# Attention and channel mix on one core: a longer search for the order of the work, and half as many dummy products

## The chip, the cores and the metric

The kernel runs on one core of one Trainium2 chip. The time is the device time of one execution, in microseconds (us). A core has five engines that run side by side, each with its own queue and strictly in that queue's order: PE (matrix products), ACT (functions of one operand, copies), DVE (elementwise work with two operands, scans), POOL (small side work) and SP (here it only starts transfers). PE shows twice in the profile: PE is the product, PEld the loading of its stationary operand.

## The reference

The first part is a linear attention with a decaying state: 4 batches, 8 heads, 768 steps, head size 48. The second part mixes each step with the one before it and sends it through a gated two-layer network with 384 features and 1,024 hidden ones.

```python
for t in range(S):
    state = alpha[:, :, t, :, None] * state + np.einsum('bhd,bhe->bhde', k[:, :, t], v[:, :, t])
    y[:, :, t] = np.einsum('bhd,bhde->bhe', q[:, :, t], state)
...
xk = mu_k * x + (1.0 - mu_k) * x_prev
xr = mu_r * x + (1.0 - mu_r) * x_prev
k = np.maximum(xk @ w_k, 0.0)
v = k * k @ w_v
r = 1.0 / (1.0 + np.exp(-(xr @ w_r)))
return (r * v).astype(np.float32)
```

All in float32; `x` is `y` with the heads side by side.

## The kernel before

**Tiles and stages.** The 768 steps of each batch are cut into chunks of 128, and the chunks into nine groups (`CUTS`, line 27): three groups of two chunks for the first batch, two groups of three for each of the others. A chunk of a group is called a unit; there are 24. For each group the kernel loads four tiles (`al`, `q`, `k`, `v`; two buffers each), runs the decay forward and backward over the group with two scans on DVE (`fwd`, line 357, and `bwd`, line 381), and multiplies q and k by them (`qm`, `km`, line 398). For each unit PE transposes k (`trans`, line 448), ACT copies the result (`keep`, line 455), and PE makes a visit (line 582): one visit finishes one unit (its products inside the chunk, and those with the old state) and starts the next (its state update and its scores). Behind a visit DVE masks the scores (`masked`, line 472) and advances the state (`advance`, line 535), ACT copies the output (`copied`) and DVE adds to it (`crossed`). Two small transfers (`moved`, line 575) complete the group's output.

Then follows the network for the group: ACT and DVE mix the steps and split the result into a high and a low part (`mix_*`, lines 604 to 620), PE makes eight first-layer products (`up`, line 628), each passed on by ACT (`relu`, `square`, `high`) and DVE (`low`); one gate product for each chunk (`gate`, line 657); and eight second-layer products for each chunk (`down`, line 672). Each product is three: high by high, high by low, low by high. The weights come in ten pieces, each split by ACT and DVE before use (`split_*`, lines 309 to 347), and four of them land in buffers that group tiles use later.

**What sets the order.** The kernel writes down all this work as jobs (line 68): engine, price in us (`COST`, line 48), what it depends on, and which buffer it opens or frees. The class `Plan` (line 63) then lays the jobs out on the host, while the program is built. `forward` (line 97) goes through time and gives each engine the ready job with the earliest latest-time; a transfer of a given size is priced by `RATE` and `LAND` (line 56). `backward` (line 155) goes from the end and gives each job the latest time at which it can start without moving the end; buffers that the forward pass found shared count as dependencies. `solve` (line 193) takes turns with both, 12 times (`PASSES`), and keeps the start times of the shortest layout. Each job has a `rank` that is added to its latest time, and it is 0 for every job. The loads are tied in a fixed order among themselves; `moved` and the stores find their own places among them in SP's queue.

The loop at line 1021 issues the jobs of all five engines in the order of the planned start times. Where the plan leaves PE empty for more than 0.7 us before a PE job, and that job starts before 60 us (`EARLY`) of the plan, it puts dummy products in front of it: `dummy(m)` (line 444) issues m products of a zero tile into a spare corner of the transposes' PSUM tile. So a dummy waits for that tile, and the next transposes wait behind the dummies.

Of the kernel before, what the change touches and what calls it, by code (L numbers as in the profile page):

```python
# [43 lines left out]
NX = HB - D  # L44
MERGE = ()
EARLY = 60.0
PASSES = 12
COST = {
    "fwd": (2.4, 3.45), "bwd": (2.32, 3.38), "am": 0.62, "adv": 0.72, "scl": 0.4, "cross": 0.42,
# [13 lines left out]
class Plan:  # L63
# [129 lines left out]
    def solve(self):  # L193
        jobs = self.jobs
        self.links = self.users()
        self.holders = {}
        for k, j in jobs.items():
            for o in j["frees"]:
                self.holders.setdefault(o, []).append(k)
        late = self.backward({k: j["n"] for k, j in jobs.items()}, ())  # L200
        best = None
        for _ in range(PASSES):
            ranked = {k: t + jobs[k]["rank"] for k, t in late.items()}
            start, span, edges = self.forward(ranked)
            self.spans = getattr(self, "spans", []) + [span]
            if best is None or span < best[0]:
                best = (span, start)
            late = self.backward(start, edges)
        self.end = {k: t + jobs[k]["cost"] for k, t in best[1].items()}
        return sorted((t, jobs[k]["n"], k) for k, t in best[1].items())  # L210

# [2 lines left out]
def gated_attention_channel_mix(  # L214
# [225 lines left out]
    def room(name):  # L440
        spare[0] = ps.tile([C, 512], F32, tag="pt", name=name)
        return spare[0][:, : NP * R].rearrange("c (p r) -> c p r", p=NP)

    def dummy(m):
        for _ in range(m):
            PE.matmul(spare[0][:R, NP * R :], zero, zero[:, : 512 - NP * R], start=True, stop=True)  # L446
# [569 lines left out]
    with tc.manual_schedule(engines={ET.PE, ET.SP, ET.Activation, ET.DVE, ET.Pool}):  # L1016
        nc.scalar.dma_start(mu, mu_p)
        DVE.tensor_scalar(nu, mu, -1.0, 1.0, op0=ALU.mult, op1=ALU.add)
        room("warm")
        busy = 0.9  # L1020
        for t, _, key in plan.solve():
            j = plan.jobs[key]
            if j["eng"] == "PE":
                if t < EARLY and t - busy > 0.7:
                    dummy(int((t - busy - 0.4) / 0.2))
                busy = t + j["cost"]
            j["fn"]()

# [2 lines left out]
    with tc.If(good < R):  # L1031
# [11 lines left out]
        with tc.For_i(0, S, TB) as t0:  # L1043
            a, k, q = (p1.tile([128, TB, DW], F32, tag=n, name="f" + n) for n in ("xrh", "pp", "kh"))
# [162 lines left out]
```

## Time and profile before

| | |
|---|---|
| time, three runs | 387.15, 388.81, 395.81 us (median 388.81) |
| the profiled execution's own time | 387.16 us |
| its span, first to last instruction | 385.4 us |
| mean granted PE clock | 0.952 |
| PE busy | 366.7 us, 95% |
| DVE busy | 240.8 us, 62% |
| ACT busy | 213.1 us, 55% |
| of PE: line 446, the dummies (76 and 246 records) | 14.4 and 35.1 us |

The page lists busy time by engine, the span in 40 equal slices with the busy share in tenths, the chain of work that ended last, and the costliest groups of instructions by line. The row PEclk gives the clock that PE was granted, in tenths. A timeline row gives start, length, engine, line and operation, output and inputs, shapes and count, and in brackets how long the engine stood idle before it and what ended that. Consecutive products overlap, so the length of one is more than the distance to the next.

### The profile page before, as it was taken

Reading aid. Unit: us, or ns where it says so; the run is one execution under the profiler, and the core shown is the slowest. Engines: PE = TensorE matmul, PEld = TensorE weight load, DVE = VectorE, ACT = ScalarE, POOL = GpSimd, SP = SyncE. Lnnn points to the kernel's source line nnn. Section 1 sums busy time; section 2 is a strip of 40 time slices with the busy share of each in tenths; the row PEclk is TensorE's granted clock in tenths of the full one; section 3 lists DMA queues with packets and bytes.
Section 4 is the critical chain, followed back from the end, with each engine's and each line's share of the span. In section 5 each row is a group of like instructions: output and inputs, shape, how many; then the busy total and the mean of one; then the engine's idle time right before and its main releaser. Section 6 shows DMA issues by size and latency. Waiting matters only on the chain.

```text
span 385.4 us, 11112 instructions
## 1 busy us (share of the span) xinstructions
PE 366.7 (95%) x4868; PEld 354.1 (92%) x4868; DVE 240.8 (62%) x399; ACT 213.1 (55%) x436; POOL 22.8 (6%) x54
## 2 busy tenths in 40 slices
PE   8998998988999999799999999999999999999993
PEld 8887997988899899799999999999999999999992
DVE  7459699768989797986788637523822452342210
ACT  2252694255558737648773578239717836826700
POOL 4000000100002000060002000000000000000000
PEclk9999599558999999899999999999999999999998
DMA  8930948912718119201901700010010010010001
GB/s 246 370 86 7 320 169 239 252 29 60 234 38 253 50 44 245 54 22 51 266 4 43 242 6 0 31 52 0 21 39 22 1 42 22 0 43 20 2 20 48
DMA packets 10999, 35.60 MB, mean 92 GB/s; under 512 B 1552, under 2 KB 5488, under 8 KB 10944
## 3 DMA queue, kind: packets, MB, share of 16 engines
q1 hardware_dynamic: 10800, 34.82, 29.6%
q8 instruction: 40, 0.66, 0.7%
q14 instruction: 15, 0.12, 0.1%
q10 hardware_dynamic: 144, 0.00, 0.0%
HBM read 28.92 MB, written 4.72 MB: 87 GB/s over the span
## 4 chain that ended last, share of the span: by engine, by line
PE 87%; DVE 5%; DMA 3%; issue 2%; ACT 1%; SPq 0%; DVEq 0%; ACTq 0%
PE pv L680 27%; PE pk L635 24%; PE pg L663 9%; PE pt L446 7%; PE warm L446 4%; PE sp L466 4%; PE yu L528 4%; PE yu L490 3%; PE pt L453 3%; DMA al<-al_p 3%; PE sp L510 2%; PE yu L510 2%; ACT ht L457 1%; DVE vraw L326 1%; DVE wvl L345 1%
## 5 line engine op out<-in xcount | busy, mean ns | idle before, releaser
L655 DVE TENSOR_TENSOR kl<-sq,kh 128x384 fp32r<-128x384 f32 (+1 forms) x72 | 36.1, 510 | 48.8 <-ACT kh L651 48.7
L680 PE MATMUL pv<-wvh,kh 128*128 128x384 f32 x192 | 66.4, 346 | 0.2 <-ACT r L642 0.2
L680 PE MATMUL pv<-wvl,kh 128*128 128x384 f32 x192 | 64.9, 338 | 0.0
L680 PE MATMUL pv<-wvh,kl 128*128 128x384 f32 x192 | 64.4, 335 | 0.0
L642 ACT ACTIVATE r<-pk 128x384 f32<-128x384 f32 (+1 forms) x72 | 32.7, 454 | 40.6 <-PE pk L635 40.4
L635 PE MATMUL pk<-xkh,wkh 128*128 128x384 f32 (+1 forms) x216 | 48.2, 333 | 0.0
L635 PE MATMUL pk<-xkh,wkl 128*128 128x384 f32 (+1 forms) x216 | 46.2, 323 | 0.0
L635 PE MATMUL pk<-xkl,wkh 128*128 128x384 f32 (+1 forms) x216 | 46.0, 322 | 0.0
L646 ACT ACTIVATE sq<-r 128x384 f32<-128x384 f32 (+1 forms) x72 | 35.3, 490 | 12.5 <-DVE kl L655 10.7
L446 PE MATMUL pt<-st 112*112 112x64 f32 x246 | 35.1, 315 | 3.1 <-ACT ht L457 3.1
L446 PEld LDWEIGHTS pt<-st 112*112 112x112 f32 x246 | 33.5, 227 | 4.9 <-ACT ht L457 4.4
L680 PEld LDWEIGHTS pv<-wvh,kh 128*128 128x128 f32 x192 | 36.0, 187 | 1.2 <-ACT r L642 0.5
L635 PEld LDWEIGHTS pk<-xkh,wkh 128*128 128x128 f32 x216 | 36.4, 194 | 0.7
L635 PEld LDWEIGHTS pk<-xkh,wkl 128*128 128x128 f32 x216 | 36.8, 194 | 0.0
L635 PEld LDWEIGHTS pk<-xkl,wkh 128*128 128x128 f32 x216 | 36.7, 193 | 0.0
L680 PEld LDWEIGHTS pv<-wvh,kl 128*128 128x128 f32 x192 | 36.1, 188 | 0.0
L680 PEld LDWEIGHTS pv<-wvl,kh 128*128 128x128 f32 x192 | 36.0, 188 | 0.0
L651 ACT ACTIVATE kh<-sq 128x384 fp32r<-128x384 f32 (+1 forms) x72 | 34.8, 488 | 2.0
L607 ACT ACTIVATE x<-xt,mu 128x384 f32<-128x384 f32 (+1 forms) x54 | 27.9, 571 | 13.4 <-DVE xrl L620 8.9
L686 DVE TENSOR_TENSOR sig<-pv,sig 128x384 f32<-128x384 f32 x24 | 13.3, 555 | 32.6 <-PE pv L680 32.5
L457 ACT COPY ht<-pt 128x448 f32<-128x448 f32 x24 | 12.7, 528 | 36.8 <-PE pt L453 31.4
L611 DVE SCALAR_TENSOR_TENSOR x<-xt,nu,x 128x384 f32<-128x384 f32 (+1 forms) x54 | 28.1, 568 | 3.0 <-ACT x L607 2.1
(84 smaller groups left out, 576.3 us busy)
## 6 DMA issues: line engine op xcount, KB each, us to landing
out<-sig SPq DMA_DIRECT2D x24, 192.0 KB, 1.9
al<-al_p SPq DMA_DIRECT2D x6, 673.8 KB, 11.2
q<-q_p SPq DMA_DIRECT2D x6, 672.0 KB, 5.0
k<-k_p SPq DMA_DIRECT2D x6, 672.0 KB, 7.1
v<-v_p SPq DMA_DIRECT2D x6, 600.0 KB, 9.2
both<-wk_p SPq DMA_DIRECT2D x4, 768.0 KB, 10.3
vraw<-wv_p SPq DMA_DIRECT2D x4, 768.0 KB, 7.9
al<-al_p SPq DMA_DIRECT2D x3, 449.8 KB, 5.6
```

Of the source, the lines that this page charges most:

```text
L446: PE.matmul(spare[0][:R, NP * R :], zero, zero[:, : 512 - NP * R], start=True, stop=True)
L457: ACT.copy(ht[u], pts[u])
L466: PE.matmul(sp[s * HC : (s + 1) * HC, j, p * HC : (p + 1) * HC], h[rr, c, p, tt], q[rr, c, p, tt], start=True, stop=True,)
L607: ACT.activation(mixed[g, i][:, t], xt[:, t, 1 : 1 + n], AF.Copy, scale=mu[:, i, t : t + 1])
L611: DVE.scalar_tensor_tensor(x, xt[:, t, 0:n], nu[:, i, t : t + 1], x, op0=ALU.mult, op1=ALU.add)
L635: PE.matmul(pk, w[:, t, cols], x[:, t], start=i == 0 and t == 0, stop=i == 2 and t == NT - 1,)
L642: ACT.activation(self.r[f], self.p["u", f], AF.Relu)
L646: ACT.activation(self.s[f], self.r[f], AF.Square)
L651: ACT.activation(self.k[0][:, f], self.s[f], AF.Copy)
L655: DVE.tensor_tensor(kl[:, f], self.s[f], kh[:, f].bitcast(F32), op=ALU.subtract)
L663: PE.matmul(pg, x[:, i, cols], w[:, i], start=k == 0 and i == 0, stop=k == 2 and i == NT - 1,)
L680: PE.matmul(pv, x[:, f, cols], w[:, f], start=f == 0 and i == 0, stop=f == NF - 1 and i == 2,)
```

## The change

Two things change. The planner's search gets 160 rounds in place of 12 passes. In every round but the first, each latest time is moved by a number between -30 and +30 us (`SHAKE`), from a generator with a fixed seed; the forward pass runs on these, and its result is then improved by a backward and a forward pass without shaking. Each of the two layouts is kept if it is the shortest so far by the planner's prices, and the next round shakes around the kept one. The first round is not shaken and gives the first two layouts of the kernel before. The rank is no longer added. And a planned gap on PE gets about half as many dummies: one for each 0.4 us in place of 0.2. No job, price, dependency or tile changes.

```diff
-PASSES = 12
+PASSES = 160
+SHAKE = 30.0
...
+        seed = 1
+
+        def shake():
+            nonlocal seed
+            seed = (seed * 1103515245 + 12345) % 2**31
+            return (seed / 2**30 - 1.0) * SHAKE
+
         late = self.backward({k: j["n"] for k, j in jobs.items()}, ())
         best = None
-        for _ in range(PASSES):
-            ranked = {k: t + jobs[k]["rank"] for k, t in late.items()}
-            start, span, edges = self.forward(ranked)
-            self.spans = getattr(self, "spans", []) + [span]
-            if best is None or span < best[0]:
-                best = (span, start)
-            late = self.backward(start, edges)
+        self.spans = []
+        for i in range(PASSES):
+            start, span, edges = self.forward({k: t + shake() if i else t for k, t in late.items()})
+            for _ in range(2):
+                if best is None or span < best[0]:
+                    best = (span, start)
+                    late = self.backward(start, edges)
+                if span == float("inf"):
+                    break
+                start, span, edges = self.forward(self.backward(start, edges))
+            self.spans.append(best[0])
         self.end = {k: t + jobs[k]["cost"] for k, t in best[1].items()}
         return sorted((t, jobs[k]["n"], k) for k, t in best[1].items())
...
                 if t < EARLY and t - busy > 0.7:
-                    dummy(int((t - busy - 0.4) / 0.2))
+                    dummy(int((t - busy - 0.5) / 0.4))
                 busy = t + j["cost"]
```

## The prediction

> **What bounds the kernel now.** I read the page's summary first, then the stretches ahead of and behind the first second-layer product, then the chain of waits with the timelines of PE and DVE in the first 100 us. The page's busy times, the granted clock in tenths, and the chain:
>
> ```profile
> PE 366.7 (95%) x4868; PEld 354.1 (92%) x4868; DVE 240.8 (62%) x399; ACT 213.1 (55%) x436; POOL 22.8 (6%) x54
> PEclk9999599558999999899999999999999999999998
> PE 87%; DVE 5%; DMA 3%; issue 2%; ACT 1%; SPq 0%; DVEq 0%; ACTq 0%
> ```
>
> PE is busy for 95% of the span, but part of that is filler. The first `down` product starts at 97.71 us. Start, length, instruction; then three window rows (window, length, busy time and count of PE, PEld, DVE, ACT, POOL; clock; DMA share; GB/s): all engines up to 97.7, line 446 on PE alone in the same stretch, and PE from there to the end.
>
> ```profile
> 97.71 0.44 PE L680 MATMUL pv<-wvh,kh 128*128 128x384 f32 x1
> 0.00:97.70 97.70, 89.48 (x1264) 84.89 (x1264) 74.64 (x105) 47.50 (x85) 8.59 (x34) 0.84 0.58 179
> 0.00:97.70 97.70, 49.60 (x322) 0.84 0.58 179
> 97.70:385.40 287.70, 277.18 (x3608) 0.99 0.21 63
> ```
>
> Line 446 is the dummy product: 49.60 of the 89.48 us are filler, and only 39.9 us are the kernel's own. From 97.7 on PE works 277.18 of 287.70 us at 0.99 of its clock with no filler at all. So the kernel is a PE-bound stretch of 288 us behind a start-up of 98 us, and neither half of the change can shorten the PE work of that stretch: what is to be had lies in the start-up.
>
> How long one dummy takes decides the rest. The tile view counts the dummies, the chain of waits has three trains of them:
>
> ```profile
> L446 PE MATMUL warm<-st x76: 394/394/449, 1.2 to 15.3; 112*112 112x64 f32 x76
> 1.22 14.45 PE warm L446 x76
> 27.57 4.89 PE pt L446 x48
> 68.39 10.60 PE pt L446 x56
> ```
>
> Every train has an even count; I read one call of the loop as two records (one fp32 product in two passes). Then the first train is 38 calls in 14.45 us, 0.38 us each; the second 24 calls in 4.89, 0.20 each; the third 28 in 10.60, 0.38 each. The old rule puts one call per 0.2 us of planned gap: right at the fast rate, and twice the gap at the slow one. In those two slow trains filler overruns its gap and holds up real work, because PE runs in order.
>
> **The change, part by part: the dummies.** The new rule is one call per 0.4 us. If the order stayed, a count of n would mean a gap of 0.2n+0.4 to 0.2n+0.6, and so 38, 2, 5, 13 and 28 calls become 18 or 19, none or 1, 2, 6 and 13 or 14. The trains that come ahead of real work, on PE:
>
> ```profile
> 15.77 0.98 PE L453 MATMUL pt<-ident,k 112*128 112x112 f32 x4
> 17.38 1.01 PE L446 MATMUL pt<-st 112*112 112x64 f32 x4 [0.62 <-ACT ht L457]
> 21.82 2.13 PE L446 MATMUL pt<-st 112*112 112x64 f32 x10 [0.62 <-ACT ht L457]
> 39.44 5.11 PE L446 MATMUL pt<-st 112*112 112x64 f32 x26
> ```
>
> And DVE, whose bracket gives idle time and what ended it:
>
> ```profile
> 5.17 2.30 DVE L362 TENSOR_TENSOR_SCAN pp<-al,fl 112x1028 f32<-112x1028 f32 x1 [0.56 <-DMA al<-al_p]
> 10.12 0.69 DVE L398 TENSOR_TENSOR k<-k,al 112x512 f32<-112x512 f32 x1
> 18.32 0.96 DVE L326 SCALAR_TENSOR_TENSOR both<-both,tops 128x768 uint32<-128x768 uint32 x1 [5.70 <-ACT tops L315]
> 27.64 0.69 DVE L475 TENSOR_TENSOR am<-sp,mask 128x512 f32<-128x512 f32 x1 [3.22 <-PE sp L466]
> 48.25 0.69 DVE L475 TENSOR_TENSOR am<-sp,mask 128x512 f32<-128x512 f32 x1 [2.23 <-PE sp L466]
> ```
>
> Head: the transposes at 15.77 need only the k product that ended at 10.81. Nineteen calls at 0.38 end at 8.4, so they start at about 10.9: 4.9 us. The four records at 17.38 nearly go (0.6 to 1.0, I take 0.9), the ten at 21.82 become four (1.3). Together 7.1 us by the masking at 27.64, in front of which DVE stood idle for PE. Does a load take it back? DVE's split at 18.32 stands ahead of the first masking in its queue, and waits through ACT for the first weight piece:
>
> ```profile
> 2.69 0.68 SPq L303 DMA_DIRECT2D both<-wk_p  x1
> both<-wk_p SPq DMA_DIRECT2D x1, 768.0 KB, 8.4
> ```
>
> Issued at 2.69 and landing 8.4 later, it is there at 11.1: not the bound at 12 or 13 us either. So 7.1 stands.
>
> Second: 26 records become 12, 2.7 us less; the masking behind that visit waits 2.23, and work queued on DVE limits the gain to that: 2.2.
>
> Third: 56 records become 26 or 28, 5.3 to 5.7 us less. The visit behind them needs a v load; an al load holds ACT. Their issues and landings (last figure, us), the visit, and the masking that follows it:
>
> ```profile
> 60.15 0.37 SPq L291 DMA_DIRECT2D v<-v_p  x1
> v<-v_p SPq DMA_DIRECT2D x1, 400.0 KB, 6.6
> 66.47 0.31 SPq L273 DMA_DIRECT2D al<-al_p  x1
> al<-al_p SPq DMA_DIRECT2D x1, 673.8 KB, 13.9
> 79.00 1.06 PE sp L466 x32
> 80.13 0.69 DVE L475 TENSOR_TENSOR am<-sp,mask 128x512 f32<-128x512 f32 x1 [3.17 <-PE sp L466]
> ```
>
> The v load is there at 66.75, well ahead of the visit at 79.00, so the visit is free to come earlier, and DVE's idle 3.17 is the most that it brings. The al load lands only at 80.4, and ACT's queue stands behind it: the least is 0, and I take half, 1.6. Dummies: 7.1 + 2.2 + 1.6 = 10.9 us.
>
> **The clock, which pays for it.** The PE rows of two bright stretches, all PE work with DVE, and line 446 alone:
>
> ```profile
> 27.70:37.90 10.20, 8.91 (x146) 8.18 (x149) 9.99 (x16) 2.54 (x6) 0.64 (x4) 1.00 0.01 2
> 48.20:68.60 20.40, 18.25 (x216) 17.31 (x216) 19.29 (x27) 14.90 (x28) 0.46 (x4) 1.00 0.70 207
> 27.70:37.90 10.20, 6.56 (x62) 1.00 0.01 2
> 48.20:68.60 20.40, 9.64 (x90) 1.00 0.70 207
> 34.50:37.92 3.42, 2.13 (x26) 0.99 0.00 0
> 68.60:72.00 3.40, 3.40 (x20) 0.50 1.01 244
> ```
>
> Dummies that follow real work run at clock 1.00, those at 68.6 at 0.50 although PE has no gap. (In the page's first slices the clock reads 9, but the 0.38 us a call there is that of the half rate; I go by the durations.) With half of them the clock may fall sooner. Real work in the two stretches is 2.35 + 8.61 = 11.0 us, so at half clock it costs 0 to 11 us. DVE is busy 9.99 of 10.20 and 19.29 of 20.40 there and hides all but its idle 1.3: I take 1.
>
> The Trainium skill (TensorE: Matmul & The Clock Gate, "Why this matters for your kernels") wants no PE idle gap above some 3 us and says that about 4 us of sustained products bring the clock up; by that rule halved filler is a mistake, the whole 11 us would be lost, and the sum below would be 382 (the clock rival). This trace half disagrees: 14.45 us of unbroken dummies stayed at 0.38 us a call and 10.60 us did so again, so here filler does not raise the clock; that it holds a raised one (the train at 27.57) fits the rule.
>
> **The new order.** The search changes the order in every queue: PE, ACT, DVE, POOL, and on SP the places of `moved` and `store` among the loads, whose own order is fixed. No operation is added, no tile changes, the rank that is dropped was 0 everywhere. The kept plan is the shortest by the planner's own prices, so the trace has to say what an order can bring. Ceiling: DVE does work for groups 3 and 4 ahead of the first `down` that nothing of group 0 needs:
>
> ```profile
> 69.65 3.37 DVE L362 TENSOR_TENSOR_SCAN pp<-al,fl 112x1540 f32<-112x1540 f32 x1 [1.77 <-DMA al<-al_p]
> 73.15 1.27 DVE L398 TENSOR_TENSOR q<-q,pp 112x512 f32<-112x512 f32 x2
> 81.61 3.36 DVE L384 TENSOR_TENSOR_SCAN al<-al,fl 112x1540 f32<-112x1540 f32 x1
> 88.75 3.36 DVE L362 TENSOR_TENSOR_SCAN pp<-al,fl 112x1540 f32<-112x1540 f32 x1
> 94.72 3.36 DVE L384 TENSOR_TENSOR_SCAN al<-al,fl 112x1540 f32<-112x1540 f32 x1
> ```
>
> Four scans, 13.5 us, and six products at 0.635, 3.8: 17 us could move behind. Floor: the planner reckons 0.34 MB/us and 2.1 us of landing (line 56), 4.1 us for an al load of 0.674 MB, where the row above has 13.9; one such load moved onto DVE's path costs 9.8. Between -17 and +10 I take -5, nearest to the idle time that DVE has left: 97.7 - 74.64 = 23.1, less 5.2 ahead of its first scan, less 10.9 counted above, is 7, of which the load waits (1.77 before the scan at 69.65) will stay.
>
> **Sum**, against the profiled execution's own 387.16 (the median of the three runs, 388.81, is 0.4% above it): 387.16 - 10.9 - 5 + 1 = 372.
>
> **Rivals.**
> - Ceiling: the order moves the whole 17 us. 387.2 - 10.9 - 17 + 1 = 360. For it: DVE is full from 48 to 68 us, so that what it does first decides. Against: behind 97.7 PE lacks 287.7 - 277.2 = 10.5 us as it is, and scans moved there must open no new gap. Chance 0.12.
> - The search does nothing: its first two candidates repeat the old ones unshaken, and if no shaken one is shorter, the old order stays with fewer dummies: 387.2 - 10.9 + 1 = 377. Chance 0.09.
> - Clock: the halved trains let it fall at once and all 11 us lie on the path: 372 + 10 = 382. For it: in the 3.42 us ahead of 37.92, after which the page shows a 5, PE was still busy for 2.13, so a clock can fall at 62% busy. Against: DVE's full rows. Chance 0.13.
> - Hidden: the freed PE time is eaten by ACT and loads at the second and third train and half of the head: 387.2 - 3.5 = 384. Against it: the idle rows of DVE above name PE. Chance 0.08.
> - Slower: loads. A planner that believes 4.1 us for a load of 13.9 packs DVE's scans against them, and DVE, in order, stands with everything behind it. At the 9.8 us missing per load, three loads (groups 3 to 8 have this size) make 372 + 29 = 401. It decides from 25 us of load waits on DVE's and ACT's path. For it: the landing row; against: loads keep their order, and of the scans quoted just one waits, 1.77. Chance 0.11.
>
> **Numbers.** Forecast 372, chance 0.47, its own range 362 to 380 (the third train 0 or 3.2, the order 0 to -12, the clock up to 5). A measurement of this kernel tells about 2% from no change, 381.0 and 396.6. Faster: forecast, ceiling and unchanged order, 0.68. Within: clock and hidden, 0.21. Slower: 0.11. From 359 to 386 all but the slower case and edges is held.
>
> **What would show it.** PE: the opening train ends near 8 us and the first transposes stand at about 11, not 15.77. DVE: the idle 3.22, 2.23 and 3.17 in front of the maskings mostly gone. The first `down` at 80 to 84 us instead of 97.7, line 446 at well under half of 49.6 us, and about 277 us of PE work behind it as now. Clock rival: 0.50 in nearly every slice until the first `down`. Wrong: a first `down` no earlier than 95, load waits of tens of us on DVE or ACT, or new PE gaps behind 100 us.

## The result and the profile after

The changed kernel takes 364.69 us (median of four runs, 361.02 to 369.04) against 387.98 us before; the ratio is 0.936, with a 95% interval of 0.928 to 0.945. The forecast was 372 in a range from 359 to 386: the direction and the range held, and the gain is about 23 us where 16 were forecast.

Some executions of every kernel run a few per cent longer, the first profiled one after among them, so the ratios leave these out while the medians hold them, and the rows "after" below are those of a second profile of the same kernel (run `e5_after`, 367.11 us, span 365.3). In the changed kernel the lines have moved by 12: the dummies are line 458, the masking 487, the scans 374 and 396, `down` 692.

The summary of the page:

```profile
span 365.3 us, 10693 instructions
PE 338.4 (93%) x4666; PEld 324.3 (89%) x4666; DVE 239.4 (66%) x399; ACT 211.2 (58%) x436; POOL 16.1 (4%) x54
PEclk9965869999999989999989999999999999999998
```

Before, PE was busy 366.7 of 385.4 us, now 338.4 of 365.3. Line 458 on PE alone, and then all of PE, in the first 100 us (window, length, busy time and count, clock, DMA share, GB/s); the last two rows are the same pair of the kernel before:

```profile
0.00:100.00 100.00, 20.79 (x120) 0.88 0.65 198
0.00:100.00 100.00, 88.02 (x1366) 0.88 0.65 198
0.00:100.00 100.00, 49.60 (x322) 0.85 0.59 182
0.00:100.00 100.00, 91.78 (x1277) 0.85 0.59 182
```

There is no filler behind 100 us in either. So the 20.1 us between the spans are: filler 49.6 to 20.8, -28.8; PE's own work (busy time less filler) 317.1 to 317.6, +0.5; PE idle 18.7 to 26.9, +8.2. And of its own work PE has done 67.2 us by 100 us, where it had done 42.2: 25 us more. Of these 25, five are lost again behind 100 us, nearly all as PE idle time, 10.5 us before and 14.9 now.

The timeline of PE and DVE after, with the rows that answer to those of the prediction: the opening train, the first transposes, the first `down`, the second masking, and the scans of groups 3 and 4.

```profile
1.22 6.98 PE L458 MATMUL warm<-st 112*112 112x64 f32 x36 [1.22 <-DVE st L727]
10.85 0.98 PE L465 MATMUL pt<-ident,k 112*128 112x112 f32 x4 [2.64 <-DVE k L410]
59.26 0.34 PE L692 MATMUL pv<-wvh,kh 128*128 128x384 f32 x1
20.50 0.68 DVE L487 TENSOR_TENSOR am<-sp,mask 128x512 f32<-128x512 f32 x1
65.35 3.37 DVE L374 TENSOR_TENSOR_SCAN pp<-al,fl 112x1540 f32<-112x1540 f32 x1 [1.48 <-DMA al<-al_p]
69.70 3.36 DVE L396 TENSOR_TENSOR_SCAN al<-al,fl 112x1540 f32<-112x1540 f32 x1
85.19 3.37 DVE L374 TENSOR_TENSOR_SCAN pp<-al,fl 112x1540 f32<-112x1540 f32 x1
89.74 3.36 DVE L396 TENSOR_TENSOR_SCAN al<-al,fl 112x1540 f32<-112x1540 f32 x1
```

The train ends at 8.2 and the transposes start at 10.85, as soon as DVE's product is there. DVE no longer stands idle ahead of the second masking (3.22 us before). The first `down` comes at 59.3 instead of 97.7, and all four long scans, which had stood ahead of it, now stand behind it.

### The profile page after: what moved, and what is told of

Same layout as the page of the kernel before. It is cut to its first block, busy times and chain, and to the rows that moved or that the text cites. A ratio compares the mean times of both kernels' runs of the same rounds, so it can differ in the third digit from the quotient of the medians.

```text
span 367.3 us, 10693 instructions
## 1 busy us (share of the span) xinstructions
PE 341.0 (93%) x4666; PEld 327.1 (89%) x4666; DVE 239.4 (65%) x399; ACT 211.5 (58%) x436; POOL 16.7 (5%) x54
## 4 chain that ended last, share of the span: by engine, by line
PE 58%; DMA 6%; DVE 6%; issue 3%; ACT 2%; SPq 1%; DVEq 0%; ACTq 0%
PE pv L692 23%; PE pk L647 20%; PE pg L675 7%; DMA al<-al_p 5%; PE yu L502 2%; PE sp L478 2%; DVE pp L374 2%; DMA xt<-xt 2%; PE yu L540 2%; PE pt L465 1%; PE sp L522 1%; PE yu L522 1%; SPq L590 1%; DVE xt L581 1%; DVE al L396 1%
## 5 line engine op out<-in xcount | busy, mean ns | idle before, releaser
L692 PE MATMUL pv<-wvh,kh 128*128 128x384 f32 x192 | 68.3, 356 | 2.1 <-ACT sig L682 1.7
L692 PE MATMUL pv<-wvl,kh 128*128 128x384 f32 x192 | 66.0, 344 | 0.0
L692 PE MATMUL pv<-wvh,kl 128*128 128x384 f32 x192 | 65.5, 341 | 0.0
L667 DVE TENSOR_TENSOR kl<-sq,kh 128x384 fp32r<-128x384 f32 (+1 forms) x72 | 35.5, 509 | 41.3 <-ACT kh L663 41.2
L663 ACT ACTIVATE kh<-sq 128x384 fp32r<-128x384 f32 (+1 forms) x72 | 34.6, 487 | 28.5 <-PE pv L692 26.9
L647 PE MATMUL pk<-xkh,wkh 128*128 128x384 f32 (+1 forms) x216 | 49.1, 338 | 0.0
L647 PE MATMUL pk<-xkl,wkh 128*128 128x384 f32 (+1 forms) x216 | 46.9, 327 | 0.0
L647 PEld LDWEIGHTS pk<-xkh,wkh 128*128 128x128 f32 x216 | 37.2, 200 | 0.7
L647 PEld LDWEIGHTS pk<-xkh,wkl 128*128 128x128 f32 x216 | 37.8, 199 | 0.0
L623 DVE SCALAR_TENSOR_TENSOR x<-xt,nu,x 128x384 f32<-128x384 f32 (+1 forms) x54 | 29.1, 569 | 8.7 <-ACT x L619 7.9
L374 DVE TENSOR_TENSOR_SCAN pp<-al,fl 112x1540 f32<-112x1540 f32 (+1 forms) x9 | 27.1, 3007 | 1.5 <-DMA al<-al_p 1.3
L396 DVE TENSOR_TENSOR_SCAN al<-al,fl 112x1540 f32<-112x1540 f32 (+1 forms) x9 | 27.0, 3003 | 0.1
```

Source lines behind the costliest of these rows:

```text
L374: DVE.tensor_tensor_scan(flat(pp), flat(al), fl[:, : NP * (n + 1)], initial=START, op0=ALU.mult, op1=ALU.max)
L396: DVE.tensor_tensor_scan(back, back, fl[:, : NP * (n + 1)][:, ::-1], initial=0.0, op0=ALU.mult, op1=ALU.max)
L623: DVE.scalar_tensor_tensor(x, xt[:, t, 0:n], nu[:, i, t : t + 1], x, op0=ALU.mult, op1=ALU.add)
L647: PE.matmul(pk, w[:, t, cols], x[:, t], start=i == 0 and t == 0, stop=i == 2 and t == NT - 1,)
L663: ACT.activation(self.k[0][:, f], self.s[f], AF.Copy)
L667: DVE.tensor_tensor(kl[:, f], self.s[f], kh[:, f].bitcast(F32), op=ALU.subtract)
```

## The experiments

Theory A is the one of the prediction: a dummy takes 0.38 us at the slow rate, so the old trains held real work up; the rest is the order. B: the order does all of it. C: filler holds the clock, and less of it costs.

**The two halves apart, and no filler at all.** The four kernels ran together, beside a kernel before of 388.48 us.

Half the dummies, old order:

```diff
-                    dummy(int((t - busy - 0.4) / 0.2))
+                    dummy(int((t - busy - 0.5) / 0.4))
```

> The order of before with the new rule for dummies alone. Theory A (a dummy takes 0.38 us at the slow rate, so the old trains overran their gaps and held real work up, and the clock costs little): 377, the opening train over at about 8 us. Theory B (the order does all of it, freed PE time is eaten elsewhere): 384 to 388. Theory C (less filler means a slower clock on the path): 385 to 395.

Measured: 380.98 us, ratio 0.980 (0.971 to 0.989). Faster, but by 7.5 us and not 11. The maskings in the old order, line 475, now read:

```profile
19.89 0.69 DVE L475 TENSOR_TENSOR am<-sp,mask 128x512 f32<-128x512 f32 x1 [1.40 <-PE sp L466]
38.38 0.69 DVE L475 TENSOR_TENSOR am<-sp,mask 128x512 f32<-128x512 f32 x1
66.38 0.68 DVE L475 TENSOR_TENSOR am<-sp,mask 128x512 f32<-128x512 f32 x1
```

They stood at 27.64, 48.25 and 80.13: 7.8, 9.9 and 13.8 us earlier. The first `down` and PE from there to the end:

```profile
83.27 0.44 PE L680 MATMUL pv<-wvh,kh 128*128 128x384 f32 x1
83.27:380.30 297.03, 280.12 (x3608) 0.97 0.22 61
```

The first `down` came at 97.71, so 14.4 us were gained up to it. Behind it the same 3,608 records take 297.0 us where they took 287.7: 9.3 us are given back, 2.9 as busy time and 6.4 as idle time. The waits of PE say what the idle time is (total us, times, longest): this kernel first, then the kernel before.

```profile
PE pt L453 <- issue: 8.5, 3, 4.1
PE pk L635 <- issue: 2.0, 1, 2.0
PE sp L466 <- issue: 1.5, 1, 1.5
```

```profile
PE sp L510 <- issue: 2.8, 2, 2.3
PE yu L510 <- issue: 1.0, 1, 1.0
```

"Issue" is idle time for which the profile names no releaser: 12.0 us against 3.8. Not all of it is of one kind. One of these waits ends 0.1 us behind DVE's product k, which the transposes need:

```profile
26.73 0.69 DVE L398 TENSOR_TENSOR k<-k,al 112x512 f32<-112x512 f32 x1
27.52 0.98 PE L453 MATMUL pt<-ident,k 112*128 112x112 f32 x4 [1.89 <-issue]
```

The other 10.1 us, all behind the first `down`, end 1.3 to 1.5 us after a 16 KB piece of PE's code has landed, as the last section shows; I call them waits for code. In the kernel before they are all of the 3.8 us, also behind the first `down`, so they account for nearly the whole 6.4 us of idle time. That is a cost that the prediction did not have; the last runs go after it. PE's own work also took longer, 346.7 - 23.5 = 323.2 us against 317.1, at a mean clock of 0.934 against 0.952.

The new order with the old rule:

```diff
-                    dummy(int((t - busy - 0.5) / 0.4))
+                    dummy(int((t - busy - 0.4) / 0.2))
```

> The new order with the old rule for dummies. Theory A: the order brings what the dummies do not, 24 of 388 less 11, so about 375; the opening train ends at 15.7 us again. Theory B: 364, as with both. Theory C: 355 to 362, for more filler holds the clock.

Measured: 373.13 us, ratio 0.959 (0.955 to 0.963), as A has it. So the order alone is worth 15 us, the dummies alone 7.5, and both together 19 to 25 (the ratios 0.950, in a later set of runs, and 0.936): within the spread they add up. PE's own work done by 100 us adds up in much the same way: 55.7 us with half the dummies alone, 55.6 with the order alone (91.14 busy less 35.50 of filler, below), 67.2 with both, 42.2 with neither.

```profile
0.00:100.00 100.00, 35.50 (x258) 0.98 0.61 181
0.00:100.00 100.00, 91.14 (x1324) 0.98 0.61 181
```

No dummies, in the new order and in the old one:

```diff
-EARLY = 60.0
+EARLY = 0.0
```

> The new order with no dummies at all. Theory A (filler does not raise the clock and holds it only where nothing of weight runs): within 4 us of the changed kernel, 360 to 367. Theory C: 370 or more, with the clock at 0.50 for most of the first 60 us. If dummies are still in the way of real work: under 360.

> The order of before with no dummies at all. Theory A: 374 to 380, at or a little under the half-filled one. Theory C: slower than the half-filled one by 5 us or more.

Measured: 366.13 us, ratio 0.946 (0.940 to 0.951), in the new order; 373.10 us, ratio 0.961 (0.956 to 0.967), in the old. In the old order no filler at all is 8 us faster than half of it, just below the range of A, and C, which expected it slower, falls. But filler is not the whole of these 8 us: waits for code make 4.6 us here and 10.1 with half the dummies. The new order's gain with no filler in either is 7 us, less than half of the 15 that it has with the old trains. Under the old rule the new order issues 35.5 us of filler where the old one issues 49.6; that the rest of the 15 comes from this is a reading that no run tests.

**The opening train, and whether the chip follows the planner.** Four kernels beside a kernel before of 389.95 us. The first is the changed kernel again, as the measure for the others.

> The changed kernel again, as the measure for the runs beside it: 0.93 to 0.95 of the kernel before, 360 to 369 us.

Measured: 367.04 us, ratio 0.950 (0.938 to 0.962).

The changed kernel without its opening train only:

```diff
-                if t < EARLY and t - busy > 0.7:
+                if 0.9 < busy and t < EARLY and t - busy > 0.7:
```

> The changed kernel without its opening train of dummies (36 records, 6.98 us ahead of the first transposes), all later ones kept. Theory A (the opening train ends before its work is ready and does not raise the clock): the same as the changed kernel within 2 us. Theory C (the opening train readies the clock for the first visits): slower by 2 to 5 us, first visits at the slow rate for longer.

Measured: 357.91 us, ratio 0.924 (0.913 to 0.934): 9 us faster, which no theory had. The train cannot have held anything up: with it the first transposes start at 10.85, without it at

```profile
11.11 0.98 PE L465 MATMUL pt<-ident,k 112*128 112x112 f32 x4 [11.11 <-DVE k L410]
```

At 43 us the kernel with the train is even 0.8 us ahead: the next dummies start at 42.18 with it and at 42.95 without. What differs comes later. All waits on "issue" with the train, and then the only one without it:

```profile
PE sp L478 <- issue: 2.8, 2, 1.7
PE pv L692 <- issue: 1.9, 1, 1.9
PE yu L522 <- issue: 1.9, 1, 1.9
PE pt L458 <- issue: 1.6, 1, 1.6
PE pt L465 <- issue: 0.5, 1, 0.5
```

```profile
PE sp L478 <- issue: 1.8, 1, 1.8
```

8.7 us against 1.8; all but the last line of the five, 0.5 us that end 0.1 behind DVE's product k, are waits for code. One wait of 1.61 ends at 45.87, inside the dummies that started at 42.18; the nine records behind it take 0.2 us each, which is the slow rate:

```profile
45.87 1.76 PE L458 MATMUL pt<-st 112*112 112x64 f32 x9 [1.61 <-issue]
```

The page's clock row above reads 6 in the slice that begins there (the sixth of 40), and without the train it reads 9:

```profile
PEclk9975899999999999999899999999999999999997
```

PE's own work is 313.0 us without the train (325.9 busy, 12.9 of it filler) and 317.6 with it. PE from 43 us to the end, with the train and then without it, and three stretches of the kernel with the train:

```profile
43.00:365.30 322.30, 302.71 (x4077) 0.97 0.26 74
43.00:356.60 313.60, 298.79 (x4085) 0.99 0.26 76
45.30:52.10 6.80, 6.23 (x49) 0.50 0.01 4
130.60:134.00 3.40, 3.40 (x13) 0.50 0.18 63
181.80:185.20 3.40, 3.40 (x58) 0.50 0.29 98
```

So the whole 8.7 us between the two spans arise behind 43 us: 4.8 as idle time, where waits for code are 7.0 against 1.8 us, and 3.9 as busy time. Three of the four waits for code there, of 1.61, 1.86 and 1.85 us, have a stretch at half the clock upon them, 13.6 us together; without the train there is one such wait, of 1.83, and one such stretch, of 3.4, ahead of the idle end. Not every wait has one (1.71 us at 107.00 has none), and that the waits bring the stretches about is argued from their places.

Less search, and another seed:

```diff
-PASSES = 160
+PASSES = 20
```

> The changed kernel with 20 rounds of search in place of 160: the planner's own length for its plan is 353.2, between 356.1 (the order of before, which took 381.0 with half the dummies) and 344.3 (160 rounds). If the length of the plan carries over to the chip: 375 to 379. If the chip does not follow the planner and the new order was a lucky one: anywhere from 362 to 385, most likely 366 to 372.

```diff
-        seed = 1
+        seed = 7
```

> The changed kernel with another seed for the shaking (7), which gives another order, of planned length 342.7. If the length of the plan carries over: 359 to 364, a little under the changed kernel. If the new order was a lucky one: 366 to 378.

Measured: 369.67 us, ratio 0.956 (0.946 to 0.967), with 20 rounds, and 361.60 us, ratio 0.935 (0.926 to 0.945), with seed 7. Another order of nearly the same planned length is as good, so the new order was no lucky find. But 369.67 us lies in the range for a chip that does not follow the planner, and 361.60 in the one for a chip that does, and the planner's length is a poor measure: against the old order with half the dummies (0.980), the first 3 us of planned gain (356.1 to 353.2) brought 2.4 points of the ratio, the next 9 us (to 344.3) 0.6 points, and the last 1.6 (to 342.7) 1.5 points, where each ratio is known to about a point. Waits for code are 10.1, 4.2, 8.1 and 4.2 us in these four kernels, and they are not in the planner's prices.

**What the opening train does.** The last four beside a kernel before of 386.54 us. First the train with as many instructions, but 4 columns in place of 64:

```diff
-    def dummy(m):
+    def dummy(m, w=512 - NP * R):
         for _ in range(m):
-            PE.matmul(spare[0][:R, NP * R :], zero, zero[:, : 512 - NP * R], start=True, stop=True)
+            PE.matmul(spare[0][:R, NP * R : NP * R + w], zero, zero[:, :w], start=True, stop=True)
...
-                    dummy(int((t - busy - 0.5) / 0.4))
+                    dummy(int((t - busy - 0.5) / 0.4), *([4] if busy == 0.9 else []))
```

> The changed kernel, with the opening train's 18 dummies cut from 64 columns to 4: as many instructions in PE's queue, little of their time. Theory D (the opening train costs because its instructions move all later ones against the 16 KB pieces in which PE's code is fetched, so that PE stands waiting for code at other places): as the changed kernel, 0.95 of before or about 367, with 6 us or more of PE idle time put down to issue, a gap of 1.5 us or more near 46. Theory E (the train's time or its effect on the clock costs): as without the train, 0.92 or 358, at most 3 us of issue.

Measured: 366.09 us, ratio 0.947 (0.942 to 0.952), with 7.7 us of waits on "issue", 7.6 of them for code, and one ends at 46.03:

```profile
1.22 6.88 PE L458 MATMUL warm<-st 112*112 112x4 f32 x36 [1.22 <-DVE st L727]
46.03 1.00 PE L458 MATMUL pt<-st 112*112 112x64 f32 x9 [0.74 <-issue]
PEclk9999989999999999998989999999999999999999
```

The time and the sum of the waits are as D has them; the wait near 46 is half of the 1.5 us that D asked for, and the four others stand at 105 to 181 us. But the test is weaker than meant: 4 columns took 6.88 us where 64 took 6.98, so the train's time did not go. Nor does it take out the clock. The row reads 9 in the first slices, but there the durations show the slow rate: three records of `up` take 0.84 us at 38.0 and 0.52 from 39.2 on. PE's own work is 318.3 us, as with the full train. What speaks against the train's own time is that either train is over 2.6 to 3.1 us before the first transposes can start, and that next to nothing is lost up to 43 us: the dummies that start at 42.95 without a train start at 42.18 with the full one and at 43.21 with the narrow one.

> Seed 7 for the shaking, without the opening train. Seed 7 with the train waited 9.5 us for issue. Theory D: the waits fall elsewhere, with no reason for a gain: 354 to 366, the issue time moved. Theory E: 9 us faster than with the train, 352 to 354.

The edits are those of the two runs above, together. Measured: 356.65 us, ratio 0.923 (0.918 to 0.928), with 2.4 us of waits on "issue". Of the 9.5 with the train, 5.4 are one wait that ends at 32.84, 0.1 us behind DVE's product k; waits for code are 4.2 with the train and 1.9 without. The time lies in D's range and above E's; the gain of the removal is 1.2 points of the ratio here, 2.6 with seed 1.

Loads priced nearer to the trace, without the opening train:

```diff
-RATE, LAND, HOP, DRAIN, SLACK = 0.34, 2.1, 0.1, 0.25, 0.12
+RATE, LAND, HOP, DRAIN, SLACK = 0.26, 4.0, 0.1, 0.25, 0.12
```

> The changed kernel without the opening train, its planner pricing loads nearer to what the traces show (0.26 MB/us and 4.0 us of landing in place of 0.34 and 2.1). If waits for loads are what the plan lost on the chip: 350 to 355. If not: 356 to 362, no better than the same kernel with the old prices (358).

Measured: 357.22 us, ratio 0.924 (0.919 to 0.929): the same as with the old prices (0.924). Pricing loads nearer to the trace gains nothing.

Dummies that are not all zero, in the kernel before (the mask of the text below holds ones on one side of a diagonal and zeros on the other):

```diff
-            PE.matmul(spare[0][:R, NP * R :], zero, zero[:, : 512 - NP * R], start=True, stop=True)
+            PE.matmul(spare[0][:R, NP * R :], ident[:R, :R], mask[:R], start=True, stop=True)
```

> The kernel before, its dummies multiplying the identity by the mask of ones in place of zero by zero; same size and count. If zeros are why the opening train stays at 0.38 us a call: after some 4 us of the train a call takes 0.20, and the train of 76 records is over in 9 to 11 us. If the kind of product is the reason: 14.4 us as before, 388 in all.

Measured: 386.69 us, and the train as slow as ever:

```profile
2.71 14.45 PE L446 MATMUL warm<-mask,ident 112*112 112x64 f32 x76 [2.71 <-POOL mask L728]
```

So it is not that all operands are zero. Most factors still are, for the identity has one value in each column that is not; a train of dense values was not tried.

The fastest versions are the three that drop the opening train and keep the later ones, 0.923 to 0.924 of the kernel before; they differ among themselves by less than their intervals, and all are faster than the changed kernel beside which the first of them ran.

## Why the prediction was right, and where it was wrong

**Filler holds up real work: right, and its price nearly so.** The step "transposes at about 10.9" was met at 10.85, and in the old order the maskings moved by 7.8 and 9.9 us where 7.1 and 9.3 were worked out. The third step, 1.6 from a span of 0 to 3.2, was too small: the masking at 80.13 came 13.8 us earlier, so that step was about 3.9, and the al load that was to hold ACT moved forward with everything else (issued at 57.27, not 66.47). The three steps, 10.9 us, were too small for what the first `down` gained, 14.4, and too large for the total, 7.5: behind the first `down` 6.4 us more of waits for code and 2.9 more of work took back a part. The sum had no term for that; the "issue 2%" in its row of the chain showed that such waits exist.

**The order: the mis-sized term.** It was put at -5 between -17 and +10, by "nearest to the idle time that DVE has left". It measured -15 under the old rule. The choice of the nearest row was the mistake: what the search did is what the ceiling described, all four scans of groups 3 and 4 moved behind the first `down`. Two misses offset each other in part: the dummies with the clock, 9.9, were over 2 us too large, and this term 10 us too small. That the sum came within 8 us of the measured time, with no term for the waits for code, is in that part luck. Only 7 us of the 15 remain when there is no filler in either order; so the terms were also not independent of the filler.

**"The kernel is a PE-bound stretch of 288 us behind a start-up of 98 us, and neither half can shorten it": wrong as a yardstick.** The first `down` came at 59.3 us, not at 80 to 84 (with the dummies alone it came at 83.27), and what follows lasts 306 us. The first `down` is a place in the order and not the end of the start-up. The measure that adds up is PE's own work done by a fixed time: 25 us more by 100 us, 5 us lost behind it, 20 in all.

**The clock: little from before to after, more in the old order.** The term was +1. From the kernel before to the changed one PE's own work grew by 0.5 us, but in the old order with half the dummies it grew by 6.1 and with none by 3.4 (320.5 us). The two profiles of the changed kernel are 2.6 us apart (320.2 and 317.6), so only the 6.1 is clear of that. The clock rival (382) fell with the runs without any filler: the one in the old order is faster than its half-filled one, the one in the new order as fast. The Trainium skill (TensorE: Matmul & The Clock Gate, "Why this matters for your kernels") asks for no gaps above some 3 us; here 11 us of an idle PE at the start cost nothing that can be seen, while in the running kernel stretches at half the clock stood behind waits of only 1.6 to 1.9 us.

**The other rivals.** The search did find other orders. Loads: the waits of DVE and ACT for them in the changed kernel (total, times, longest):

```profile
DVE q L410 <- DMA q<-q_p: 4.1, 3, 2.6
DVE pp L374 <- DMA al<-al_p: 2.5, 3, 1.5
DVE k L410 <- DMA k<-k_p: 2.3, 3, 1.2
ACT junk L382 <- DMA al<-al_p: 11.7, 7, 2.8
ACT tops L327 <- DMA rraw<-wr_p: 1.5, 1, 1.5
```

They are 22.1 us, a little under the 25 at which the slower case was to decide, but the same waits made 18.8 in the kernel before, so the change added 3.3 and not the 29 of that case. What grew is ACT's wait for the two small transfers of `moved`, 15.1 us where it was 0.9, which no rival named.

The ceiling (360) was close: the first measurement lies halfway between it and the forecast.

## What to carry to other kernels

Before filling gaps on an in-order engine, measure how long one filler instruction takes at the rate that it will run at, and try the kernel with none: filler that overruns its gap is a wait like any other. Work done by a fixed time is a better yardstick than the time of a landmark, once the order may change. And where a change shifts an engine's instruction stream, look at its idle time without a releaser on both sides before believing a difference of a few per cent: what dropping 18 dummies brought here came, by the account above, from where the pieces of code fall, and need not come again in another kernel.

## What the runs showed of the hardware

**Code has to arrive.** One queue brings pieces of 16 KB that are marked as instructions: 40 in the kernel before, 38 in the changed one, 37 and 38 in the two without dummies. Their number goes roughly with that of PE's records (4,868, 4,666 and 4,546), so I take them for PE's code. The wait that ends at 107.0 in the changed kernel, and the queue's row from 104.3 to 105.6 us, in which the piece starts:

```profile
107.00 0.39 PE L478 MATMUL sp<-q,k 48*64 48x64 f32 x10 [1.71 <-issue]
q8 instruction: 1, 0.02, 5.4%
```

The piece starts at 104.39 and has landed at 105.52; PE, idle since 105.29, goes on 1.48 us later. The same holds for the other waits in this kernel: pieces that landed at 17.23, 44.55, 128.51 and 179.96 us are followed by PE at 18.69, 45.87, 129.85 and 181.43, 1.3 to 1.5 us behind. In all profiles together, the waits on "issue" end 1.2 to 1.7 us behind a piece, but for one of 0.6 us and for those of transposes that end 0.1 behind DVE's product k. With 38 pieces in 365 us, a place taken at random would lie there about one time in twenty (an estimate from these two numbers). Most pieces cost nothing: the changed kernel has 38 of them and five such waits. Single waits for code are 0.3 to 4.1 us long and make 1.8 to 10.1 us in one kernel or the other. The Trainium skill (Runtime: NRT & Kernel Launch, "Instruction fetch mechanics") has code streamed in blocks of 16 KiB while the engine works, with the cost of a block boundary mostly hidden; here 10.1 us of a run of 380 were not hidden. They moved when 18 dummies in front were removed, and came back near the same places when the dummies came back with fewer columns. Why one piece is late and another is not stays open.

**A product of 4 columns costs as much as one of 64.** 36 dummies with 4 columns took 6.88 us and with 64 columns 6.98: about 0.19 us a record either way. In the narrow train the load of the stationary tile takes 307 ns and the product 327 (minimum/median/maximum, ns). The load takes 307 in the wide train too; whether it sets the pace is not shown.

```profile
L458 PEld LDWEIGHTS warm<-st x36: 259/307/307, 1.2 to 7.7; 112*112 112x112 f32 x36
L458 PE MATMUL warm<-st x36: 327/327/347, 1.2 to 7.8; 112*112 112x4 f32 x36
```

**Not every busy PE raises the clock.** 14.45 us without a gap stayed at the slow rate, with zeros and with the identity and the mask alike. Each record loads a tile of 112 columns and streams 64 columns through it; whether so little streaming is the reason was not tried.
